# A planned whole-kernel order with eight single PSUM banks: attention reads feeding a max-out FFN on one core

## The chip, the cores and the metric

The kernel runs on one core of one Trainium2 chip. The metric is device time in microseconds for one execution; three executions of the kernel before took 152.25, 152.40 and 152.42 us, a median of 152.4. The profile comes from one more execution. Names of engines: PE is the matmul engine (PEld its weight loads), DVE the vector engine, ACT the scalar engine, POOL the general engine, SP the engine that only issues transfers. POOL also issues transfers, those that change the type among them.

## The reference

Eight batches `b`, eight heads `h`, 512 tokens and 32 states per head, head width 64; then an FFN of width 768 over all 4608 output rows.

```python
scores = scale * np.matmul(x, state.transpose(0, 1, 3, 2))      # [8, 8, 512, 32]
a = softmax(scores)                                             # over the 32 states
xread = np.matmul(a, state)                                     # [8, 8, 512, 64]
a2 = softmax(scale * np.matmul(state, x.transpose(0, 1, 3, 2))) # over the 512 tokens
sread = np.matmul(a2, x)                                        # [8, 8, 32, 64]
x = concat([xread, sread], axis=2) -> [8 * 544, 512]
h = np.maximum(np.maximum(x @ w1, x @ w2), x @ w3)              # 512 -> 768
out = h @ w_out                                                 # 768 -> 512
```

Weights and inputs are float32 in DRAM, and so is the result. The kernel works in bf16 with float32 sums.

## The kernel before, in words

The read of the states is never formed for the 512 tokens of a batch: since `xread @ w = a @ (state @ w)`, the kernel computes `G = state @ w` per batch (32 states by 3 x 768 per head) and multiplies the turned softmax weights `aT` by `G`. Per batch the steps are these, each a small function named by a short word in a table:

- `lx`, `lxg`: load `x` of a batch with a change to bf16 (POOL issues). `xtd`: turn it by a DMA transpose on SP's queue into `xT` (batches 0 and 1 are turned on PE by `xt`, and copied by `xtc`).
- `lst`, `stc`, `stt`, `stp`: load, cast and turn the states of two batches and place them in `bd`, block-diagonal (one `bd` serves two batches). `stt` is four PE transposes.
- `sc`: scores, 16 matmuls with `xT` as weights and `bd` as the moving side. `ex`: exponential on ACT into `e`. `sum`: row sums and reciprocals on DVE. `wt`: the product `a` on POOL. `atd`: DMA transpose of `a` into `aT`.
- `pad`: POOL copies `x` into `xp` with a column of ones between heads. `sr`, `srs`, `srt`, `ap`: the read for the states (`e` as weights, `xp` moving), its scaling on DVE, a DMA transpose, and a copy to its place in `atp`.
- `g`, `gr`, `gq` and `gc`, `grc`, `gqc`: pieces of `G` on PE and their copies out of PSUM on ACT or DVE. Eight matmuls of a piece use eight tiles of 64 x 32 of the PE array at once.
- `l1 b m`: for one of the six 128-wide slices `m` of the FFN, 3 x 2 matmuls of 512 columns into three PSUM banks. `m0` (ACT) casts the first bank, `ma` and `mb` (DVE) take the maximum with the second and the third; `mb` writes `ht`.
- `l2 b j`: six matmuls of 512 columns into one bank, `l2c` copies it to `osb`, `so` stores it. For batch 7 there are narrower pieces (`l2p`, `l2pc`, `sop`).
- `l1s`, `l2 s`: the same for the 256 rows of the states of all batches (256 columns), at the end.
- `look`, `flag`, `vl`: a test that no sum under- or overflowed, and a branch to a slower exact path, which is not taken here. `hold` is a matmul and a copy at the end that keep the branch behind the last work.
- `busy`: matmuls on zeros during the load at the start.

The order of the work is written by hand in a string, `PLAN`: every engine works through its own steps in that order, with waits put in where data or a buffer needs them. Two more strings say which PSUM bank each use takes (`BANKS`) and which SBUF buffer (`PLACES`). Before the change PSUM has four single banks and two pairs; scores and large pieces of `G` take a pair and are copied with one instruction of 1024 columns. In the steady part one batch after another passes with the same pattern: layer 1 of batch `b`, layer 2 of batch `b-1` and the scores and `G` of batch `b+1` interleaved.

Line numbers in the profile before: L249 `busy`, L261 `stt`, L305 `sc`, L313 `ex`, L358 `at`, L391 `sr`, L427 all pieces of `G`, L444, L466 and L469 their copies, L477 layer 1, L492 `m0`, L497 `ma`, L505 `mb`, L514 `l2`, L526 its copy, L532 and L537 the narrower pieces, L543, L548, L541, L556 stores, L591 and L593 `hold`.

Of the kernel before, what the change touches and what calls it, by code (L numbers as in the profile page):

```python
# [9 lines left out]
F32 = mybir.dt.float32  # L10
# [8 lines left out]
    lst 0 A; lxu 0 0 S; zero; clr 0; clr 1; clr 2; clr 3; warm; lxg 0 1; busy 1; xones 1; ident; busy 1;  # L19
    lxg 1 0; busy 1; busy 1; stc 0 D; busy 1; busy 1; busy 1; busy 1; busy 1; lxg 1 1; stt 0; busy 1; busy 1;  # L20
    cxu 0 0 D; xt 0 0; stp 0 A; busy 1; xt 0 1; lw 0 2 1; lw 0 1 0; xtc 0 0 D; sc 0 0; xones 0; lw 0 2 2;
    xtc 0 1 D; busy 1; busy 1; sc 0 1; xt 1 0; ex 0 0; ex 0 1; lw 1 3 0; sum 0 0; sum 0 1; xtc 1 0 A; busy 1;
    busy 1; xt 1 1; sc 1 0; xtc 1 1 D; ex 1 0; busy 1; busy 1; sc 1 1; lw 2 3 2; wt 0 1 D; lw 2 3 1; lw 3 4 0;
    wt 0 0 P; lw 3 6 2; at 0 0; sr 0; ex 1 1; sr 1; g 0 0; sum 1 0; wt 1 0 P; g 1 0; atc 0 0 A; at 0 1; at 1 0;
    gc 0 0 A; atc 0 1 A; g 1 1; sum 1 1; gc 1 0 D; atc 1 0 A; srs 0; srs 1; g 0 1; wt 1 1 P; at 1 1; gc 0 1 A;
    l1 0 0; atc 1 1 D; lst 1 A; m0 0 0; lst 3 A; gc 1 1 A; ma 0 0; lw 3 6 1; lw 4 6 0; lxg 2 1; lxg 2 0; l1 0 1;
    m0 0 1; lwo; mb 0 0; g 0 2; g 1 2; ma 0 1; l1 1 0; lst 2 A; gc 0 2 A; mb 0 1; m0 1 0; ma 1 0; l1 0 2;
    mb 1 0; gc 1 2 A; m0 0 2; ma 0 2; l1 1 1; m0 1 1; g 1 3; stc 1 P; mb 0 2; ma 1 1; g 0 3; mb 1 1; stt 1;
    gc 1 3 A; l1 1 2; gc 0 3 A; m0 1 2; stp 1 DA; ma 1 2; g 0 4; g 0 5; l1 0 3; gc 0 5 D; g 1 4; mb 1 2;
    gc 0 4 A; m0 0 3; gc 1 4 A; ma 0 3; gr 2 1792 2304; mb 0 3; l1 1 3; m0 1 3; grc 2 1792 2304 A; xtd 2;  # L30
    ma 1 3; l1 0 5; stc 2 P; g 1 5; gr 2 0 512; mb 1 3; m0 0 5; ma 0 5; l1 1 4; gc 1 5 A; gr 2 1280 1792;
    m0 1 4; grc 2 0 512 D; mb 0 5; gr 2 512 1024; ma 1 4; grc 2 1280 1792 AD; l1 0 4; m0 0 4; ma 0 4; stt 2;
    mb 0 4; sc 2 -; ex 2 -; grc 2 512 1024 D; stp 2 AD; stc 3 D; mb 1 4; l2 0 3; l2 0 0; l2c 0 3 A; l2c 0 0 A;
    sum 2 -; l2 0 1; ones; pad 2; lxg 3 0; lxg 3 1; wt 2 - P; stt 3; xtd 3; l2c 0 1 A; l1 1 5; pad 3;
    so 0 0 2 P; lx 4; m0 1 5; l2 0 2; ma 1 5; mb 1 5; stp 3 A; l2c 0 2 A; l2 1 0; gq 2 1024 1280; gr 3 0 512;
    gr 3 1792 2304; l2c 1 0 D; grc 3 1792 2304 D; gqc 2 1024 1280 A; grc 3 0 512 A; atd 2; sr 2; l2 1 1; srs 2;
    sc 3 -; l1 2 0; m0 2 0; ex 3 -; l2c 1 1 D; l2 1 3; ma 2 0; gq 3 1024 1280; so 0 2 4 P; gqc 3 1024 1280 A;
    l2c 1 3 A; gr 3 512 1024; gr 3 1280 1792; mb 2 0; sum 3 -; wt 3 - P; atd 3; xtd 4; srt 0; sr 3; srs 3;
    l1 2 1; m0 2 1; ma 2 1; l1 2 2; m0 2 2; mb 2 1; ma 2 2; l1 2 3; m0 2 3; mb 2 2; ma 2 3; l1 2 5; m0 2 5;
    mb 2 3; l2 1 2; grc 3 1280 1792 A; grc 3 512 1024 A; ma 2 5; mb 2 5; l2c 1 2 D; l1 2 4; so 1 2 4 P; m0 2 4;  # L40
    ma 2 4; lx 5; mb 2 4; so 1 0 2 P; pad 4; gr 4 1792 2304; gr 4 0 512; grc 4 1792 2304 AD; l2 2 0; l2 2 1;
# [38 lines left out]
    1032103210 3213201321 0312013201 3201320120 3120132103 1203120312 0310321031 2013210321 0321032132 0132103120  # L80
    1320132103 2103120120 1201320123 0123120123 0213012013 0130123102 2
"""
PAIRS = """
    0101010101 1001010010 0110101010 1010101010 10
"""
PLACES = """
# [657 lines left out]
```

## Time and profile before

| | before |
|---|---|
| time, median of three (lowest to highest) | 152.4 us (152.25 to 152.42) |
| span of the profiled execution, first to last instruction | 150.5 us |
| what lies around the span, median less span | 1.9 us |
| PE busy | 145.1 us, 96% of the span |
| DVE busy | 118.0 us, 78% |
| ACT busy | 83.2 us, 55% |
| POOL busy | 56.1 us, 37% |
| granted PE clock | 1.000 over the span |

The profiled execution's own time is not listed apart from its span; the three timed ones lie 1.75 to 1.92 us above it. How to read it: PE counts as busy from a matmul's start to its modelled end, and matmuls overlap, so that 96% says only that PE seldom stands empty. The chain that ended last, followed back from the end, tells which work has no slack. The windows view cuts the span into stretches and shows for each how long an engine was busy.

### The profile page before, as it was taken

How to read it: one execution, taken by the hardware profiler on the slowest of the kernel's cores; microseconds unless marked ns; L12 is line 12 of the kernel's file. 1: busy time of each engine (PE TensorE's matmuls, PEld its weight loads, DVE VectorE, ACT ScalarE, POOL GpSimd, SP SyncE). 2: the span in 40 equal slices, each digit the busy share in tenths (PEclk: the TensorE clock that was granted, in tenths of full speed). 3: DMA queues.
4: the chain of work that ended last, by engine and by line, in shares of the span. 5: the costliest groups of instructions: out<-in, count | busy, mean ns of one | idle time of the engine just before them, and what ended most of it. 6: DMA issues, size and time to landing. Idle time of an engine off the chain costs nothing.

```text
span 150.5 us, 3618 instructions
## 1 busy us (share of the span) xinstructions
PE 145.1 (96%) x1422; PEld 72.8 (48%) x1422; DVE 118.0 (78%) x202; ACT 83.2 (55%) x144; POOL 56.1 (37%) x78
## 2 busy tenths in 40 slices
PE   6998999999999999999999999999999999999991
PEld 2556443335444443444344434443444446689770
DVE  6488788999967899789978997899789888674443
ACT  3366888965654574457546764676466653332220
POOL 6996911090392507350735064506250200001500
PEclk9999999999999999999999999999999999999999
DMA  4999999949647996998399839983303340300555
GB/s 121 195 188 189 206 230 198 196 97 139 124 97 171 235 182 189 108 209 178 145 102 216 183 139 90 231 183 131 157 4 78 121 175 7 139 0 17 190 199 167
DMA packets 39108, 22.29 MB, mean 148 GB/s; under 512 B 23072, under 2 KB 36896, under 8 KB 39088
## 3 DMA queue, kind: packets, MB, share of 16 engines
q0 software_dynamic: 15872, 13.96, 49.3%
q1 hardware_dynamic: 21632, 6.69, 22.8%
q10 hardware_dynamic: 1584, 1.38, 3.2%
q8 instruction: 12, 0.20, 0.6%
q14 instruction: 8, 0.07, 0.2%
HBM read 15.20 MB, written 8.91 MB: 160 GB/s over the span
## 4 chain that ended last, share of the span: by engine, by line
PE 88%; DMA 5%; POOL 3%; issue 1%; DVE 1%; ACT 1%; POOLq 0%
PE pw L477 47%; PE po L514 25%; PE pg L427 6%; DMA w<-in_moe_w_dram 5%; PE po L532 4%; PE ps L305 2%; PE psr L391 2%; POOL w L217 1%; POOL x L206 1%; PE pgh L427 1%; ACT G L444 1%; PE pt L261 1%; DVE held L593 0%; PE idle L591 0%; PE pat L358 0%
## 5 line engine op out<-in xcount | busy, mean ns | idle before, releaser
L477 PE MATMUL pw<-aT,G 128*128 128x512 bf16 x288 | 66.7, 379 | 0.0
L492 ACT CAST t<-pw 128x512 bf16<-128x512 f32 (+1 forms) x54 | 30.5, 564 | 27.3 <-PE pw L477 26.4
L497 DVE TENSOR_TENSOR t<-t,pw 128x512 bf16<-128x512 bf16 (+1 forms) x54 | 35.3, 654 | 11.1 <-ACT t L492 8.9
L477 PEld LDWEIGHTS <-G 128*128 128x128 bf16 x288 | 27.1, 98 | 32.8 <-issue 2.1
L514 PE MATMUL po<-wout,ht 128*128 128x512 bf16 x168 | 39.7, 379 | 0.0
L505 DVE TENSOR_TENSOR ht<-t,pw 128x512 bf16<-128x512 bf16 x48 | 32.9, 686 | 4.5
L349 POOL TENSOR_TENSOR a<-e,rden 128x1024 bf16<-128x1024 bf16 (+1 forms) x9 | 14.6, 1622 | 27.2 <-ACT osb L526 11.1
L514 PEld LDWEIGHTS <-ht 128*128 128x128 bf16 x168 | 15.4, 98 | 19.0 <-issue 1.7
L548 POOL DMA_DIRECT2D out_dram<-osb x13 | 7.4, 571 | 27.5 <-ACT t L492 27.5
L466 ACT CAST G<-pg 128x1024 bf16<-128x1024 f32 (+1 forms) x17 | 14.7, 895 | 2.1 <-PE pg L427 2.1
L526 ACT COPY osb<-po 128x512 f32<-128x512 f32 x15 | 8.9, 592 | 9.1 <-PE po L514 9.1
L526 DVE COPY osb<-po 128x512 f32<-128x512 f32 x14 | 9.6, 688 | 3.9 <-PE po L514 3.8
L375 POOL COPY xp<-x 128x1024 bf16<-128x1024 bf16 x12 | 12.3, 1059 | 0.0
L313 ACT ACTIVATE e<-ps 128x1024 bf16<-128x1024 f32 (+1 forms) x10 | 8.5, 854 | 6.7 <-PE ps L305 6.7
L466 DVE CAST G<-pg 128x1024 bf16<-128x1024 f32 (+1 forms) x12 | 11.6, 995 | 0.0
L342 DVE TENSOR_REDUCE seen<-e 128x32 f32<-128x1024 bf16 (+1 forms) x10 | 10.0, 997 | 1.7 <-ACT e L313 1.7
L427 PE MATMUL pg<-w,bd 64*32 64x512 bf16 (+1 forms) x288 | 10.7, 362 | 0.4 <-DMA w<-in_moe_w_dram 0.2
L444 ACT CAST G<-pg 128x768 bf16<-128x768 f32 x10 | 8.0, 810 | 2.7 <-PE pg L427 2.5
L543 POOL DMA_DIRECT2D out_dram<-osb x4 | 2.2, 544 | 19.4 <-ACT osb L537 19.4
L249 PE MATMUL idle<-zero 128*128 128x512 bf16 x18 | 7.4, 506 | 1.8 <-DVE zero L225 1.3
L477 PE MATMUL pw<-atp,w 128*128 128x256 bf16 x72 | 8.7, 272 | 0.0
L217 POOL DMA_DIRECT2D w<-in_moe_w_dram x10 | 7.7, 782 | 0.0
(70 smaller groups left out, 112.1 us busy)
## 6 DMA issues: line engine op xcount, KB each, us to landing
out_dram<-osb POOLq DMA_DIRECT2D x12, 512.0 KB, 3.7
x<-in_x_dram POOLq DMA_DIRECT2D x4, 512.0 KB, 7.2
x<-in_x_dram POOLq DMA_DIRECT2D x7, 256.0 KB, 5.8
w<-in_moe_w_dram POOLq DMA_DIRECT2D x4, 256.0 KB, 7.5
w<-in_moe_w_dram POOLq DMA_DIRECT2D x2, 384.0 KB, 7.5
wout<-in_moe_w_out_dram POOLq DMA_DIRECT2D x1, 768.0 KB, 12.0
out_dram<-osb SPq DMA_DIRECT2D x3, 256.0 KB, 2.4
stf<-in_state_dram ACTq DMA_DIRECT2D x4, 128.0 KB, 5.3
```

What stands on the lines that cost most here:

```text
L342: nc.vector.reduce_sum(out=den, in_=parity(e[b], g), axis=AX.X)
L349: times[c](out=parity(a[b], g).rearrange("p j g s n -> p j (g s) n"), in0=parity(e[b], g).rearrange("p j g s n -> p j (g s) n"), in1=rdens ...
L375: nc.gpsimd.tensor_copy(out=xp[b][:, :, :, g * (D + 1):g * (D + 1) + D], in_=v[:, g])
L427: nc.tensor.matmul(p(s, g), bd(b, 2 * s + g)[64 * g:64 * g + 64, g, :], f(w_sb[64 * g:64 * g + 64, s]), start=True, stop=True, tile_positi ...
L444: copier[c[g]](out=G[b][:, g:h, :, m * 128:m * 128 + 128], in_=p[:, g:h, 0:384].rearrange("p g (i f) -> p g i f", i=3))
L466: copier[c[g]](out=v[:, g:h], in_=p[:, g:h, 0:c1 - c0])
L477: nc.tensor.matmul(pw[i][:, 0:n], lhs(i, k), rhs(k), start=(k == 0), stop=(k == nk - 1))
L492: nc.scalar.copy(out=t0s[b, m][:, 0:n], in_=open_ps["l", b, m][0][:, 0:n])
L497: nc.vector.tensor_max(t1s[b, m][:, 0:n], t0s.pop((b, m))[:, 0:n], open_ps["l", b, m][1][:, 0:n])
L505: nc.vector.tensor_max(ht[b][:, m, :], t1s.pop((b, m))[:, 0:n], open_ps.pop(("l", b, m))[2][:, 0:n])
L514: nc.tensor.matmul(p, ht[b][:, m, tokens(b, j)], wout_sb[:, m, :], start=(m == 0), stop=(m == NM - 1))
L526: copier[c[i]](out=o[:, j, i * w:i * w + w], in_=p[:, i * w:i * w + w])
```

## The change

The functions change little, the three tables wholly. What it does:

- PSUM is eight single banks. Scores and pieces of `G` take two of them, and each is copied by its own instruction (512 or 384 columns where 1024 or 768 stood).
- Batches 5, 6 and 7 are scored the other way round (`sq`, `eq`, `etd`): `bd` are the weights and `xT` moves, 16 matmuls on eight 64 x 32 tiles, so that states lie on the partitions; the exponential goes to `eT`, and a DMA transpose on SP makes `e`.
- States 4 to 7 are turned by a DMA transpose on SP (`std` for `stt`), and placed by DVE and POOL.
- `x` of batches 5, 6 and 7 is loaded by three transfers that POOL issues one after another.
- The flag's matmul and test come earlier; batch 7 is put out in seven pieces (sixteen quarter-tiles in twelve before), the first half of the states in one (two before).
- The first loads of weights are smaller; `xp` has two columns of ones.

```diff
 PLAN = """
-    lst 0 A; lxu 0 0 S; zero; clr 0; clr 1; clr 2; clr 3; warm; lxg 0 1; busy 1; xones 1; ident; busy 1;
...
+    lxg 0 1; lxu 0 0 S; zero; busy 1; lst 0 A; busy 1; busy 1; warm; busy 1; stc 0 A; busy 1; cxu 0 0 A; ident;
...
 BANKS = """
-    0123012301 2230210020 1121020310 2321302130 1203102301 2310213012 3120132132 3102301230 2301203103 2103120132
...
-PAIRS = """
...
+    0123456701 2345670234 5610275634 0721653075 1263471052 6731067450 2316475167 0253461374 2065174036
...
     def bank(shape, dtype, name):
-        return pp.tile(shape, dtype, tag="b" + next(homes["b"]), bufs=1, name=name)
-
-    def two_banks(shape, dtype, name):
-        return pp.tile(shape, dtype, tag="w" + next(homes["w"]), bufs=1, name=name)
+        return pp.tile(shape, dtype, tag="b" + next(homes[0]), bufs=1, name=name)
...
     def exps(b, g=None):
         new(e, b, [128, J, 2, HS, Ns], "e")
-        nc.scalar.activation(
-            out=parity(e[b], g).rearrange("p (c i) g s n -> p i c (g s n)", i=2),
-            in_=open_ps.pop(("s", b, g)).rearrange("p (i c) g s n -> p i c (g s n)", i=2),
-            func=AF.Exp, scale=scale)
...
+            for i in range(2):
+                nc.scalar.activation(
+                    out=out[:, i], in_=ps[i].rearrange("p c g s n -> p c (g s n)"), func=AF.Exp, scale=scale)
...
     def scores_turned(b):
-        p = open_ps["sq", b] = two_banks([128, 2, 2, 2, 128], F32, "pst")
+        ps = open_ps["sq", b] = [bank([128, 2, 2, 128], F32, "pst") for _ in range(2)]
         for g in range(2):
             for s in range(HS):
                 for c in range(2):
                     nc.tensor.matmul(
-                        p[32 * s:32 * s + 32, c, :, g, :], bd(b, 2 * s + g)[64 * c:64 * c + 64, c, :],
+                        ps[c][32 * s:32 * s + 32, :, g, :], bd(b, 2 * s + g)[64 * c:64 * c + 64, c, :],
                         xT[b][64 * c:64 * c + 64, 2 * s + g, :, :],
                         start=(g == 0), stop=(g == 1), tile_position=(64 * c, 32 * s), skip_group_check=True)
...
     def g_run(b, c0, c1):
+        ps = open_ps["g", b, c0] = [bank([128, 512], F32, "pg") for _ in range(2)]
+        g_mm(b, lambda s, g: ps[g][32 * s:32 * s + 32, 0:c1 - c0],
              lambda v: v.rearrange("p i f -> p (i f)")[:, c0:c1])
...
     def g_ran(b, c0, c1, c):
         new_g(b)
+        v = G[b].rearrange("p g i f -> p g (i f)")
+        for g, p in enumerate(open_ps.pop(("g", b, c0))):
+            copier[c[g % len(c)]](out=v[:, g, c0:c1], in_=p[:, 0:c1 - c0])
```

What the new table moves is shown at three places. The first is POOL at the start: its loads of `x` (x_82 and x_83 are batches 0 and 1) and of the three weight matrices (`w`; 128x4x128 is one 128-wide slice of one matrix), and its products `a`. Before:

```order
L206 DMA x_83<-in_x_dram 128x4x256 x2
L217 DMA w<-in_moe_w_dram 128x4x256
L217 DMA w<-in_moe_w_dram 128x4x128
L236 MEMSET x_82 128x64
L217 DMA w<-in_moe_w_dram 128x4x256 x2
L217 DMA w<-in_moe_w_dram 128x4x128 x3
L349 TENSOR_TENSOR a<-e,rden 128x4x128
L217 DMA w<-in_moe_w_dram 128x4x384
L349 TENSOR_TENSOR a<-e,rden 128x4x128 x2
L217 DMA w<-in_moe_w_dram 128x4x384
L217 DMA w<-in_moe_w_dram 128x4x256
```

Now, at the same place on POOL:

```order
L199 DMA x_83<-in_x_dram 128x4x256 x2
L210 DMA w<-in_moe_w_dram 128x4x128 x2
L210 DMA w<-in_moe_w_dram 128x4x256
L210 DMA w<-in_moe_w_dram 128x4x128 x3
L210 DMA w<-in_moe_w_dram 128x4x256
L353 TENSOR_TENSOR a<-e,rden 128x4x128
L210 DMA w<-in_moe_w_dram 128x4x128 x2
L353 TENSOR_TENSOR a<-e,rden 128x4x128 x2
L210 DMA w<-in_moe_w_dram 128x4x384
L210 DMA w<-in_moe_w_dram 128x4x256 x2
```

The three transfers that the first piece of `G` needs are four slices together where they were five; the transfers behind the products are one of 384 and two of 256 where they were two of 384 and one of 256, of which one stood between the products.

The second place is DVE in layer 1 of batch 2 (t1 is written by `ma`, ht by `mb`, osb by the copy of layer 2, sr by `srs`). Before, each slice's two maxima follow each other:

```order
L497 TENSOR_TENSOR t1_1035<-t0_1033,pw1_1025 128x512
L505 TENSOR_TENSOR ht_976<-t1_1035,pw2_1026 128x512
L497 TENSOR_TENSOR t1_1049<-t0_1046,pw1_1038 128x512
L505 TENSOR_TENSOR ht_976<-t1_1049,pw2_1039 128x512
L497 TENSOR_TENSOR t1_1063<-t0_1060,pw1_1052 128x512
L505 TENSOR_TENSOR ht_976<-t1_1063,pw2_1053 128x512
```

Now, on DVE in layer 1 of the same batch:

```order
L487 TENSOR_TENSOR t1_1071<-t0_1054,pw1_1046 128x512
L516 COPY osb_898<-po_977 128x512
L495 TENSOR_TENSOR ht_1085<-t1_1071,pw2_1047 128x512
L487 TENSOR_TENSOR t1_1087<-t0_1083,pw1_1059 128x512
L487 TENSOR_TENSOR t1_1093<-t0_1091,pw1_1075 128x512
L495 TENSOR_TENSOR ht_1085<-t1_1087,pw2_1060 128x512
L495 TENSOR_TENSOR ht_1085<-t1_1093,pw2_1076 128x512
L487 TENSOR_TENSOR t1_1126<-t0_1108,pw1_1100 128x512
L487 TENSOR_TENSOR t1_1140<-t0_1119,pw1_1111 128x512
L495 TENSOR_TENSOR ht_1085<-t1_1140,pw2_1112 128x512
```

The maxima of different slices are mixed, and a copy of layer 2 stands inside a slice. In the new plan PE meets eight slices of layer 1 in a row there (six of batch 2 and two of batch 3, with the scores of batch 4 among them); before there were at most four.

The third place is the end of ACT, before it reads the flag. Before:

```order
L537 COPY osb_2313<-po_2417 128x128
L543 DMA out_0_dram<-osb_2313 128x128
L537 COPY osb_2434<-po_2427 128x256
L537 COPY osb_2313<-po_2438 128x256
L543 DMA out_0_dram<-osb_2313 128x256
L543 DMA out_0_dram<-osb_2313 128x128 x2
```

Now, at the end of ACT (osb_2480 is the states' output, osb_2434 that of batch 7):

```order
L531 DMA out_0_dram<-osb_2480 32x4x512
L527 COPY osb_2434<-po_2492 128x384
L527 COPY osb_2434<-po_2500 128x256
L533 DMA out_0_dram<-osb_2434 128x256
L533 DMA out_0_dram<-osb_2434 128x128
```

The last two copies of the kernel are now both on ACT, and a store that waits for a copy on DVE stands ahead of them; before, the last copies were on DVE.

More of the change, by code (lines that the diff above doesn't have):

```diff
@@ L34 @@
[L34 to L38, printed above, removed]
@@ L165 @@
     open_ps = {}
-    homes = {n: iter("".join(t.split())) for n, t in (("b", BANKS), ("w", PAIRS))}
+    homes = [iter("".join(BANKS.split()))]
     places = {}
@@ L385, in sread @@
                     if b in xp:
-                        both = xp[b][:, s, j, g * D:g * D + D + 1]
+                        both = xp[b][:, s, j, g * (D + 1):g * (D + 1) + D + 1]
                     else:
```

236 lines of the change are left out of this document (115 added, 121 removed), and 3 rows, old and new, of the table BANKS.

## The prediction

> **What bounds the kernel now.** I read the page first (busy shares, chain by engine), then the windows by batch, then the chain in order of time, then the engines' own order in one batch.
>
> The page's first lines and its chain by engine; below them the windows view (columns: stretch, length, busy us and instructions of PE, PEld, DVE, ACT, POOL, granted clock, share of the DMA engines, GB/s) for the start and one batch of the steady part:
>
> ```profile
> span 150.5 us, 3618 instructions
> PE 145.1 (96%) x1422; PEld 72.8 (48%) x1422; DVE 118.0 (78%) x202; ACT 83.2 (55%) x144; POOL 56.1 (37%) x78
> PE 88%; DMA 5%; POOL 3%; issue 1%; DVE 1%; ACT 1%; POOLq 0%
> ```
>
> ```profile
> 0.00:15.90 15.90, 13.67 (x199) 7.68 (x200) 11.11 (x24) 8.31 (x14) 13.19 (x24) 1.00 1.24 174
> 79.79:95.03 15.24, 15.24 (x149) 6.81 (x150) 12.88 (x21) 9.06 (x16) 6.03 (x7) 1.00 0.83 157
> ```
>
> PE is 88% of the chain. In the steady batch PE is full, DVE has 12.88 of 15.24 us, ACT 9.06, POOL 6.03. So the end is set by three things: when PE's unbroken run begins, how much it holds, and what follows it. The chain in order of time (start us, length us, what) gives all three, and the price of each kind of PE work:
>
> ```profile
> 6.06 7.41 DMA w<-in_moe_w_dram
> 15.55 0.33 PE pat L358 x4
> 15.88 2.59 PE pw L477 x12
> 34.06 0.22 PE pt L261 x4
> 38.64 0.22 PE pt L261 x4
> 61.74 0.47 PE ps L305 x16
> 63.50 0.23 PE pgh L427 x8
> 63.73 0.43 PE pg L427 x16
> 64.54 5.30 PE pw L477 x24
> 135.09 0.33 PE po L532 x6
> 136.74 2.97 PE po L532 x36
> 142.34 0.66 PE po L532 x6
> 144.29 2.67 PE po L532 x36
> 146.95 0.02 issue
> ```
>
> The first layer-1 slice starts at 15.88, PE runs without a break of note to 146.95, and 3.55 us follow to the span's end at 150.5. Before the run, the chain is the third load of weights, 7.41 us from its issue to its landing at 13.47.
>
> **The change, part by part.** I work it out against the span of 150.5; the median is 1.9 us more (what lies around the span), which I leave as it is.
>
> *Start.* The first piece of `G` waits for three loads. They and the loads ahead hold one slice of one matrix less (128 KB in bf16), and that is also the difference up to the fifth load, which the last piece ahead of layer 1 needs. The transfers between 10 and 20 us in the DMA view:
>
> ```profile
> DMA packets 4397, 1.98 MB, mean 198 GB/s; under 512 B 2168, under 2 KB 4396, under 8 KB 4396
> ```
>
> At 198 GB/s, 128 KB are 0.65 us. Before, four transposes of `a` (0.33, the row at 15.55) stood ahead of layer 1; now batch 1's eight stand behind its first slice. So layer 1 begins 0.65 + 0.33 = 0.98 earlier, and 0.66 come into the run: net -0.32. Bounds: 0 if ACT's and DVE's copies, not the weights, hold the first slice (then only the order of the transposes changes), -0.98 if the transposes behind the first slice fill a wait.
>
> *Turning of states.* Eight PE transposes go, two rows of 0.22: -0.45. Instead SP issues two transposes, and DVE and POOL place them. The states' loads land long before, and `bd` of batches 4 and 5 is first needed at a piece of `G` some 2 us of PE work after SP is through; cost zero, else the lateness of SP below.
>
> *Scores of 5, 6, 7.* 16 matmuls of 64 columns with 128 x 128 weights go, 0.47 each batch. In come 16 of 256 columns on eight tiles at once. No such row exists before; the nearest is the pair of large `G` pieces in the same tiling, 16 of 512 columns in 0.43, so half the columns are 0.22. All three stand directly ahead of `G` pieces of the same 64 x 32 tiling, so no change of tiling comes with them. 3 x (0.47 - 0.22) = -0.75; the other bound is zero, if a tile's two sums run one after the other without overlap.
> What follows them is longer: two exponentials, a transpose on SP, then sums, product, transpose of `a`. With these rows (page and DMA issues):
>
> ```profile
> L313 ACT ACTIVATE e<-ps 128x512 bf16<-128x512 f32 x4 | 2.4, 597 | 2.5 <-PE ps L305 2.5
> L342 DVE TENSOR_REDUCE seen<-e 128x32 f32<-128x1024 bf16 x6 | 7.3, 1217 | 1.4 <-ACT e L313 1.4
> L349 POOL TENSOR_TENSOR a<-e,rden 128x1024 bf16<-128x1024 bf16 x6 | 11.4, 1908 | 25.8 <-ACT osb L526 11.1 <-ACT t L492 6.1 <-DVE seen L401 4.7
> xT<-x SPq DMA_TRANSPOSE x6, 5.3
> aT<-a SPq DMA_TRANSPOSE x6, 2.9
> ```
>
> 2 x 0.6 + 2.9 (the transpose of `e` has `a`'s eight blocks) + 1.2 + 0.35 + 1.9 + 2.9 = 10.5 us from the scores to a batch's first slice. Between them the new PE order has, for batch 5, ten slices of layer 1 or 2 (12.9), thirteen pieces of `G`, the other scores and four reads for the states: over 16 us. So this costs nothing unless SP is late.
>
> *Output.* The narrow pieces cost 0.33 + 2.97 + 0.66 + 2.67 = 6.63 for 84 matmuls. The new ones: three of 128 at 0.33, one of 256 at 0.66, one of 384 at 0.99, three of 512 (one the states') at 1.29, half of the twelve matmuls in 2.59: 6.51, so -0.12. That narrow pieces are no dearer by column than wide ones is what these rows show.
>
> *Changes of tiling.* 24 layer-1 matmuls behind `G` and `sr` take 5.30, twelve alone 2.59: 0.12 on leaving a tiled group, and as much on entering (eight of 256 columns 0.23, where half of the next row's 0.43 per eight would be 0.11). Counting the groups behind the first slice, 16 become 17: +0.24.
>
> *Single banks.* The copies of 1024 columns become two of 512. From the groups by form:
>
> ```profile
> L466 ACT CAST G<-pg 128x1024 bf16<-128x1024 f32 x12 | 11.7, 1024 | 0.0
> L466 DVE CAST G<-pg 128x1024 bf16<-128x1024 f32 x7 | 8.5, 1217 | 0.0
> L466 DVE CAST G<-pg 128x512 bf16<-128x512 f32 x5 | 3.4, 684 | 0.0
> L526 DVE COPY osb<-po 128x512 f32<-128x512 f32 x14 | 9.6, 688 | 3.9 <-PE po L514 3.8
> ```
>
> A copy in two costs DVE 2 x 0.684 - 1.217 = 0.15 more, ACT (by the exponential's 0.597, also 512 columns out of PSUM) 2 x 0.597 - 1.024 = 0.17. On DVE, seven copies of 1024 and two of 768 become twelve of 512 and ten narrower ones, some 3 us more; its output copies fall from 14 of 0.69 and seven narrow ones to 12, some 3 us less, so DVE keeps its 118. ACT gets 18 split copies (3 us) and five more output copies, less what DVE and POOL take from it: some 5 more, 88 of 150. Neither total binds; what can bind is a stretch, below.
>
> *Flag early, `x` of 5 to 7 together.* The flag's matmul only moves. The three loads are issued while POOL has 25.8 us of idle time ahead of its products (the row of L349), and the scores that need the first of them come some 20 us of PE work later. Zero both.
>
> *End.* Before, the last narrow copies were 0.29 on DVE and the last store landed 1.8 after its issue. Now ACT copies 384 and then 256 columns and issues two stores, and a store of 768 KB from POOL starts some 4 us earlier. The rows that bear on it:
>
> ```profile
> L537 ACT COPY osb<-po 128x256 f32<-128x256 f32 x3 | 1.1, 374 | 0.7 <-PE po L532 0.7
> out_dram<-osb POOLq DMA_DIRECT2D x12, 512.0 KB, 3.7
> out_dram<-osb ACTq DMA_DIRECT2D x3, 64.0 KB, 1.8
> ```
>
> The copy is 0.08 longer and the last store stands behind another (about 0.3 of issue): between -0.4 (eight last stores where there were fourteen) and +0.8 (the large store in the way); I take +0.3, what the two rows give.
>
> *New waits.* The states' load (issue to landing), and SP's queue (start, time that it holds SP):
>
> ```profile
> stf<-in_state_dram ACTq DMA_DIRECT2D x4, 128.0 KB, 5.3
> ```
>
> ```profile
> 80.39 2.97 SPq L291 DMA_TRANSPOSE xT<-x  x1
> 83.46 1.25 SPq L366 DMA_TRANSPOSE aT<-a  x1
> 84.80 1.19 SPq L410 DMA_TRANSPOSE ats<-sr  x1
> ```
>
> The states of 2 and 3 are loaded one transfer later on ACT and turned earlier, by the start's 0.98 and some 0.9 of PE work. The load takes 5.3, so `stt` may wait 0 to 0.5. SP is fuller: between the transposes of `x` of 5 and 6 stand two small ones and, ahead, that of `a` of 4. SP holds 2.97 for each `x`, 1.25 for `a`, 1.19 for each small one: 2 x 2.97 + 2 x 1.19 + 1.25 = 9.6, and 2.3 more to landing; PE has some 11 us of work from the product `a` of batch 4 to the scores of batch 6. Just short: 0 to 1. For all new waits I take +0.4, between 0 and 3.1 (the DVE case below).
> [...]
>
> Sum: -0.32 - 0.45 - 0.75 - 0.12 + 0.24 + 0.3 + 0.4 = -0.7. Span 149.8, time **151.7 us**.
>
> **The rivals.**
>
> *The start is given back* (about no change). The weights of the fourth slice come in a transfer that POOL issues only after its products `a` of batch 1, as before. If that load, not PE, sets when those pieces of `G` run, PE waits there for what it gained (0.65 to 0.98). For it: the start's window has the DMA engines full (share 1.24). Against: the queue ahead is shorter. Time: 152.4 - 0.7 + 0.7 = 152.4.
>
> *Slower: DVE in two long runs of layer 1.* Three steps of DVE in a steady batch (start, length), and the group of the first reduction of `look`:
>
> ```profile
> 65.73 0.69 DVE L497 TENSOR_TENSOR t<-t,pw 128x512 bf16<-128x512 bf16 x1 [0.42 <-ACT t L492]
> 66.53 0.69 DVE L505 TENSOR_TENSOR ht<-t,pw 128x512 bf16<-128x512 bf16 x1
> 67.13 0.68 DVE L497 TENSOR_TENSOR t<-t,pw 128x512 bf16<-128x512 bf16 x1
> ```
>
> ```profile
> L566 DVE TENSOR_REDUCE top<-seen 128x1 f32<-128x272 f32 x1 | 0.4, 427 | 0.0
> ```
>
> Eight slices and one set of scores in a row in batches 2 and 3 are 8 x 1.29 + 0.47 = 10.8 of PE; DVE has 16 maxima, a copy and a scaling, 16 x 0.685 + 0.69 + 0.4 = 12.0. Ten in a row in batches 5 to 7 are 12.9 of PE against 20 x 0.685 + 1.15 (`look`: two reductions of 0.43 and two small tests) = 14.85. The excess is 1.2 + 1.9 = 3.1. Eight banks hold two slices and two thirds, so a part is absorbed, but DVE enters the first run with sums and copies of `G` still to do. What decides is DVE's pace from start to start, in the rows above 0.80 where `mb` needs the `ma` ahead of it, 0.60 where it doesn't. The new order mixes slices, so most steps should take 0.60, and then 16 of them are 9.6 and the run fits. If the pace stays 0.685 or worse, the price is 3.1 less 0.8 that the banks take: 151.7 - 0.4 + 2.3 = 153.6.
> [...]
>
> *Faster: nothing new waits.* All terms but the end and the waits are -1.4, and 0.4 of the start's other 0.66: 150.6. For it: PE is the chain in 88%, and the mixed order suits DVE. Against: every queue is fuller.
>
> **How the numbers follow.** Forecast 151.7 (its own range 151.0 to 152.1): 0.42. Faster still, 150.6: 0.14. No change, 152.4: 0.17. Slower, 153.6: 0.27. Within 0.2%, 0.3 us, nothing can be told from no change. So faster 0.56, same 0.17, slower 0.27. The range for 8 in 10 reaches from the gain with no waits, the start at its bound and the end 0.4 shorter, 152.4 - 1.4 - 0.66 - 0.4 = 149.9, to the DVE case in which the banks take only 0.5, 151.3 + 2.6 = 153.9.
>
> **What would show it.** Right: the chain's first layer-1 slice near 14.9; rows of `pst` of 0.2 to 0.25 for 16; PE's run ending near 146 and 3.8 us behind it; steps of 0.60 between DVE's maxima. Wrong: PE idle or waiting on DVE between 48 and 60 or 100 and 115 us; PE waiting on the weights near 21; a transposed `x` or `e` that lands after PE asks for it; DMA engines full to the last microsecond.

## The result: 5.6% slower, and the profile after

| | before | after |
|---|---|---|
| time, median (lowest to highest) | 152.4 us (152.25 to 152.42) | 160.7 us (159.99 to 161.81, four executions) |
| ratio, with its 95% interval | | 1.056 (1.051 to 1.061) |
| span of the profiled execution | 150.5 us | 159.6 us (its own time 161.35) |

The forecast was 151.7, its range ended at 153.9. Some kernels below have executions far above their fastest; the ratios leave those out, and there the text gives lowest and highest. The page of the changed kernel: its first lines, PE's busy tenths and the granted clock in forty slices of 4 us, and the chain by engine.

```profile
span 159.6 us, 3543 instructions
PE 147.2 (92%) x1381; PEld 71.2 (45%) x1381; DVE 112.2 (70%) x204; ACT 86.2 (54%) x170; POOL 56.8 (36%) x79
...
PE   6999999999999999999998942899999999999980
...
PEclk9999999999999999999999998589999999999999
...
PE 78%; DMA 8%; ACT 3%; DVE 3%; POOL 2%; SPq 2%; issue 1%; ACTq 0%; DVEq 0%
```

PE has a hole in slices 23 to 25, counted from 0, and just behind it the clock falls. PE's own rows there (start, length, group; in brackets its idle time before and what ended it), its first slice of layer 1 and its last output:

```profile
14.92 1.46 PE L467 MATMUL pw<-aT,G 128*128 128x512 bf16 x6
...
87.25 0.41 PE L326 MATMUL pst<-xT,bd 64*32 64x256 bf16 x16 [0.55 <-DMA xT<-x]
...
98.42 1.07 PE L395 MATMUL psr<-xp,e 128*32 128x65 bf16 x64 [4.90 <-DMA e<-eT]
100.16 6.49 PE L467 MATMUL pw<-aT,G 128*128 128x512 bf16 x18 [0.67 <-DMA aT<-a]
...
152.93 1.79 PE L522 MATMUL po<-wout,ht 128*128 128x384 bf16 x12
```

And the windows around it (as in the prediction, the clock is the third number from the end):

```profile
96.00:100.00 4.00, 1.07 (x64) 0.91 (x64) 0.86 (x4) 0.00 (x0) 1.72 (x1) 0.79 1.13 170
100.00:104.00 4.00, 3.84 (x10) 1.37 (x11) 1.68 (x3) 0.21 (x1) 2.09 (x2) 0.50 0.15 34
104.00:108.00 4.00, 4.00 (x18) 1.70 (x17) 3.04 (x7) 2.13 (x5) 0.23 (x1) 0.86 0.34 78
```

These rows make up the 9.1 us of span:

- Start: first slice at 14.92 for 15.88, -0.96.
- Waits: 0.55 for `xT` of batch 7, 4.90 for `e` of batch 7, 0.67 for `aT` of batch 5: +6.12.
- Clock: the first 18 matmuls of layer 1 of batch 5 take 6.49. At 0.216 each (2.59 for twelve before) they'd take 3.89: +2.60. The reads ahead of them take 1.07, where the kernels below at full clock have 0.72; these 0.35 are in the last line.
- End: from PE's last output (152.93 + 1.79 = 154.72) to the span's end 4.88, before 3.55: +1.33.
- All other work of PE: from first slice to last output 139.80, before 131.07; less 6.12 and 2.60, 0.0 (and -0.35 without the reads' clock).

Why the transposes are late stands first in SP's queue (start, time that SP is held):

```profile
78.07 1.75 SPq L339 DMA_TRANSPOSE e<-eT  x1
79.92 4.12 SPq L284 DMA_TRANSPOSE xT<-x  x1
84.08 3.21 SPq L414 DMA_TRANSPOSE ats<-sr  x2
87.34 0.58 SPq L538 DMA_DIRECT2D out_dram<-osb  x1
88.01 1.10 SPq L414 DMA_TRANSPOSE ats<-sr  x1
89.22 4.65 SPq L339 DMA_TRANSPOSE e<-eT  x2
93.92 5.05 SPq L370 DMA_TRANSPOSE aT<-a  x2
```

SP is held almost without a break from 78 to 99. The transposes of `e` of 6 and 7 come at 89.2, behind `x` of 7, three small transposes and a store; that of `a` of 5 comes behind them, at 93.92. POOL's product for it was done at 87.54, 6.4 us earlier. The transfers from 88 to 101 us, in forty steps of 0.325 us, with the times from issue to landing, and POOL's rows, its product `a` of batch 5 and its issue in the middle:

```profile
GB/s 0 265 384 244 14 0 0 136 206 106 0 0 1 9 9 186 406 403 403 403 416 392 423 429 251 228 129 117 210 170 256 207 223 54 269 95 104 286 103 0
...
out_dram<-osb POOLq DMA_DIRECT2D x2, 512.0 KB, 4.4
...
e<-eT SPq DMA_TRANSPOSE x2, 6.3
aT<-a SPq DMA_TRANSPOSE x2, 4.7
```

```profile
85.63 1.91 POOL L353 TENSOR_TENSOR a<-e,rden 128x1024 bf16<-128x1024 bf16 x1 [5.99 <-DVE seen L405]
...
91.53 1.11 POOL L538 DMA_DIRECT2D out_dram<-osb  x2
```

POOL issues 1 MB of stores at 91.5, and from 93 to 96 us the engines move about 400 GB/s, while the three transposes that PE needs are under way; `e` of 6 and 7 and `a` of 5 take 4.8, 7.7 and 6.2 us (before, `aT` took 2.9). So after the result there were four candidates: SP's order, POOL's stores, POOL's pads (which the chain of waits names between 87.6 and 91.6), and the order of PE and DVE behind the late thing.

### The profile page after: what moved, and what is told of

The parts are those of the page before. It is cut to its first block, busy times and chain, and to the rows that moved or that the text cites. A ratio compares the mean times of both kernels' runs of the same rounds, so it can differ in the third digit from the quotient of the medians.

```text
span 159.6 us, 3543 instructions
## 1 busy us (share of the span) xinstructions
PE 147.2 (92%) x1381; PEld 71.2 (45%) x1381; DVE 112.2 (70%) x204; ACT 86.2 (54%) x170; POOL 56.8 (36%) x79
## 4 chain that ended last, share of the span: by engine, by line
PE 78%; DMA 8%; ACT 3%; DVE 3%; POOL 2%; SPq 2%; issue 1%; ACTq 0%; DVEq 0%
PE pw L467 43%; PE po L504 19%; PE pg L431 5%; DMA xT<-x 5%; DMA aT<-a 4%; PE idle L242 4%; PE po L522 3%; POOL xp L379 2%; SPq L339 2%; PE ps L303 1%; DVE seen L346 1%; PE psr L395 1%; PE pat L362 1%; ACT bd L264 1%; PE pst L326 1%
## 5 line engine op out<-in xcount | busy, mean ns | idle before, releaser
L459 ACT CAST G<-pg 128x512 bf16<-128x512 f32 (+1 forms) x39 | 19.5, 561 | 2.9 <-PE pg L431 2.8
L516 ACT COPY osb<-po 128x512 f32<-128x512 f32 x19 | 11.2, 588 | 12.1 <-PE po L504 12.0
L459 DVE CAST G<-pg 128x512 bf16<-128x512 f32 (+1 forms) x21 | 12.5, 629 | 2.3 <-PE pg L431 2.2
L538 POOL DMA_DIRECT2D out_dram<-osb x11 | 6.1, 558 | 20.7 <-DVE osb L516 12.5
L431 PE MATMUL pg<-w,bd 64*32 64x512 bf16 (+2 forms) x336 | 12.0, 350 | 0.1
L419 POOL COPY atp<-ats 128x128 bf16<-128x128 bf16 x4 | 1.9, 465 | 21.9 <-DMA ats<-sr 21.8
L210 POOL DMA_DIRECT2D w<-in_moe_w_dram x12 | 9.1, 783 | 0.0
L447 ACT CAST G<-pg 128x384 bf16<-128x384 f32 x18 | 7.7, 490 | 1.7 <-PE pg L431 1.6
L516 DVE COPY osb<-po 128x512 f32<-128x512 f32 x10 | 6.7, 685 | 1.7 <-PE po L504 1.7
L467 PEld LDWEIGHTS <-w 128*128 128x128 bf16 x72 | 7.0, 98 | 1.7
```

Source lines behind the costliest of these rows:

```text
L431: nc.tensor.matmul(p(s, g), bd(b, 2 * s + g)[64 * g:64 * g + 64, g, :], f(w_sb[64 * g:64 * g + 64, s]), start=True, stop=True, tile_positi ...
L459: copier[c[g % len(c)]](out=v[:, g, c0:c1], in_=p[:, 0:c1 - c0])
L467: nc.tensor.matmul(pw[i][:, 0:n], lhs(i, k), rhs(k), start=(k == 0), stop=(k == nk - 1))
L516: copier[c[i]](out=o[:, j, i * w:i * w + w], in_=p[:, i * w:i * w + w])
```

## The experiments

All kernels are edits of the changed one, and its line numbers hold. The time is the median; the ratio is to the kernel before, 152.0 to 152.3 in the same sessions.

### What the hole is

**hole_busy**

```diff
+    busy 20;   # ahead of
     sr 7; sr 6;
```

> Twenty matmuls on zeros (4.3 us at 0.215 each) stand between the last piece of G of batch 7 and the read for the states of batch 7, where PE stands empty for 4.9 us; nothing else changes. Theory (the hole has two prices, the wait for the transposes and the clock that falls while PE is empty): the matmuls cost nothing, the granted clock stays at 1.00 from 100 to 104 us (0.50 in the changed kernel), the first 18 matmuls of layer 1 of batch 5 take 3.9 instead of 6.49, and the time falls by 2.5 to 3.5 us, to 157.2 to 158.2 from 160.7. Rival (those matmuls are slow because their operands come late, not for the clock): no change, 160 to 161.8. If the transposes landed later for it: slower.

157.9, ratio 1.040 (1.037 to 1.042). PE's rows:

```profile
94.82 4.49 PE L242 MATMUL idle<-zero 128*128 128x512 bf16 x19
99.46 0.72 PE L395 MATMUL psr<-xp,e 128*32 128x65 bf16 x64
100.11 4.06 PE L467 MATMUL pw<-aT,G 128*128 128x512 bf16 x18
```

The read isn't earlier (99.46 for 98.42), yet it takes 0.72 for 1.07, the 18 matmuls take 4.06, not 6.49, and 2.7 us are gone. The granted clock is 1.00 from 100 to 104 us, where it was 0.50. The clock is a price of its own, on top of the wait.

**old_scores**

```diff
-    sq b; eq b; etd b;         # b = 5, 6, 7
+    sc b -; ex b -;
-    e ... 5:0 6:1 7:0;
+    e ... 5:0 6:2 7:1;
```

> Batches 5, 6 and 7 are scored as before the change (xT as weights, exponential straight into e, no transpose of e on SP); the buffer of e for batch 6 and 7 is a third one and the second, so that ACT needn't wait for the read of batch 4. Everything else is the changed kernel's. Theory (the transposes of e on SP's queue, with what stands ahead of and behind them, make the hole): PE gains 3 x 0.25 = 0.75 us of matmuls, the hole of 6.1 us and the slow clock's 2.6 go, 152.5 to 154.0. Rival (the late x of 7 or the stores make the hole, with or without e): a hole of at least 4 us stays between 85 and 104 us, 157 or more. Rival (the single banks or the new order elsewhere cost the time): 158 or more, with no hole there.

152.96, ratio 1.006 (1.003 to 1.009): 7.7 us hang on the turned scores and their three transposes of `e`.

```profile
93.62 0.72 PE L395 MATMUL psr<-xp,e 128*32 128x65 bf16 x64
94.27 4.06 PE L467 MATMUL pw<-aT,G 128*128 128x512 bf16 x18
```

The read and layer 1 follow without a gap: without the turned scores there is no hole. The single banks, the turned states and the three loads together are all in this kernel, and make none. Of the 0.9 us left over the kernel before, another end gives back 0.6 (below).

### What makes the transposes late

**xt7_early, stores_late, stores_xt7**: each cause alone, then both.

```diff
-    ...; etd 5; ...; xtd 7;
+    xtd 6; xtd 7; ...; etd 5;                                # xt7_early, stores_xt7
-    l1 5 5; so 3 2 4 P; ...; so 2 2 4 P; ...; wt 7 - P;
+    l1 5 5; ...; wt 7 - P; so 3 2 4 P; so 2 2 4 P;           # stores_late, stores_xt7
```

> The transpose of x of batch 7 is issued directly behind that of batch 6 (near 74 us) instead of behind the transpose of e of batch 5 (79.9); nothing else moves. Theory (SP's queue in its order makes e of 6 and 7 late): e of 5, which stood ahead of it, is issued up to 3 us later, the four small transposes, the store and e of 6 come up to 4 us earlier, e of 7 some 2 us earlier (it then waits for its scores and for the product of batch 5), and the hole shrinks from 4.9 by 2 to 3.5 us: 156.0 to 158.5, the slow clock included. Rival (POOL's pads 7 and 6 hold back e of 7, as the chain names them): e of 7 is issued no earlier than 91.6, and the time stays within 0.7 us of 160.7.

155.1 (154.5 to 155.9, and one execution at 165.6); ratio 1.021 (1.017 to 1.025). One place on SP is worth 5.6 us in most executions, more than expected. The profile is of the one at 165.6 and doesn't show the usual one: there `e` of batch 5, now behind `x` of 7, makes PE wait 2.85 us at its read, and `aT` of 5 another 4.77.

> POOL issues the two stores of 512 KB (batches 3 and 2, second halves) behind its product of batch 7 (after 100 us) instead of at 91.5; nothing else moves. In the changed kernel the DMA engines move nothing from 91.4 to 92.3, then 420 GB/s to 95.9, while the transposes of e of 6 (issued at 89.2), e of 7 (90.7) and a of 5 (93.9) are under way. Theory (those stores, issued and moved in the middle of the transposes, hold them up): e of 7 lands near 95 instead of 98.4, aT of 5 near 96 instead of 100.1, the hole shrinks by 3 to 4 us and the clock falls less: 155.0 to 157.5. Rival (the order on SP alone, or POOL's pads, set when e of 7 is issued and lands): within 0.7 us of 160.7.

156.0 (154.4 to 157.3), ratio 1.022 (1.015 to 1.029). The same window as above, and PE, in the execution at 157.3:

```profile
e<-eT SPq DMA_TRANSPOSE x2, 4.6
aT<-a SPq DMA_TRANSPOSE x2, 2.8
```

```profile
95.74 0.72 PE L395 MATMUL psr<-xp,e 128*32 128x65 bf16 x64 [1.61 <-DMA e<-eT]
96.73 5.75 PE L467 MATMUL pw<-aT,G 128*128 128x512 bf16 x18 [0.27 <-DMA aT<-a]
```

With nothing changed on SP, `e` lands in 4.6 for 6.3 and `aT` in 2.8 for 4.7: the stores did hold the transposes up, by 1.7 and 1.9 us at the median. How the transfers of POOL and of SP share the engines isn't shown.

> Both moves: the two stores late, and the transpose of x of batch 7 directly behind that of batch 6. The second alone gave 155.1 in most executions and 165.6 in one. Theory (two causes in one chain, SP's order ahead of e of 6 and 7 and the stores behind it): the hole falls below 1 us and stays there, 151.5 to 153.5, with no execution over 155. Rival (the early transpose of x of 7 collides with others whatever the stores do): the spread of several us stays.

155.0 (154.3 to 155.5), ratio 1.019 (1.015 to 1.023): the spread is gone as expected, the time is not. The two gains don't add. Part of what is left shows on other engines:

```profile
84.34 0.31 DVE L419 COPY atp<-ats 128x128 bf16<-128x128 bf16 x1 [3.07 <-DMA ats<-sr]
```

```profile
85.01 0.58 ACT L516 COPY osb<-po 128x512 f32<-128x512 f32 x1 [3.19 <-DMA out_dram<-osb]
```

A small transpose and a store now stand behind `x` of 7 on SP; DVE and ACT wait 3 us each for them, with copies of `G` and maxima behind. PE's own waits between 84 and 97 us are short, 0.92 and 0.32 for `e` and 0.35 for a copy of `G`; another part is the end, which this kernel still has as changed (4.87 us behind PE's last output, 3.77 in `queues_3` below). This run also clears POOL's pads: SP is done with both transposes of `e` at 92.16 (89.47 + 2.69), the pads run to 93.91 (91.90 + 2.01).

```profile
89.47 2.69 SPq L339 DMA_TRANSPOSE e<-eT  x2
```

```profile
91.90 2.01 POOL L379 COPY xp<-x 128x1024 bf16<-128x1024 bf16 x2
```

**sp_relief**

```diff
-    ...; so 1 0 1 S; so 1 2 4 S; ...; so 1 1 2 S; ...; srt 0; ...; srt 1; so 0 0 1 S;
     so 0 2 4 S;                                                                   # at 52 us
+    srt 0; srt 1; so 1 0 1 S; so 1 2 4 S; so 1 1 2 S; so 0 0 1 S;
```

> Six issues of SP whose data has been ready since 15 to 50 us (the small transposes of the states' reads of batches 0 and 1, and four stores of batches 0 and 1, 5.9 us of SP's time between 74 and 88 us) go to SP's idle time behind 52.6 us. Nothing else moves; the transposes of e stay, and so do POOL's stores at 91.5. Theory (SP works in order and is full from 66 to 100 us, so that what stands ahead of the transposes of e and a is what PE waits for): e of 6 is issued near 83 to 85 instead of 89.2, e of 7 as soon as its exponential is done (89) instead of 90.7 to 91.6, a of 5 near 91; PE's wait at the read for batch 7 falls from 4.9 to 1 to 2.5, the clock holds better, 153.5 to 156.5. Rival (POOL's stores and the engines' traffic at 92 to 96 alone decide): 159 or more.

160.2, ratio 1.055 (1.052 to 1.058): no better than the change. But the waits are others:

```profile
73.56 4.06 PE L467 MATMUL pw<-aT,G 128*128 128x512 bf16 x18 [2.23 <-DMA aT<-a]
...
96.26 0.71 PE L395 MATMUL psr<-xp,e 128*32 128x65 bf16 x64 [0.19 <-DMA e<-eT]
99.63 5.75 PE L467 MATMUL pw<-aT,G 128*128 128x512 bf16 x18 [2.66 <-DMA aT<-a]
```

The wait for `e` fell from 4.90 to 0.19, but only half of that is the theory's: `e` was there 2.2 us earlier (96.26 for 98.42), and PE came to the read 2.5 us later (96.06 for 93.53). The wait came back twice: for `aT` of 5 (with POOL's stores beside it again), and at 71 us for `aT` of 4. The stores had gone among the loads of `x` of 5 to 7, which then landed after 15.2 us, and the transposes of `a` beside them after 5.4; in the changed kernel they took 9.0 and 2.7:

```profile
x<-in_x_dram POOLq DMA_DIRECT2D x3, 512.0 KB, 15.2
```

So the rival that SP alone decides falls too: SP's idle time is not free time of the DMA engines.

### What stands behind the late transposes

**reads_late, all_moved, all_moved_2**

```diff
-    etd 6; ...; sum 6 -; ...; etd 7; ...; sr 7; sr 6; atd 5; l1 5 5; ...; l1 5 2; ...; l1 5 1; l2 4 1;
+    atd 5; etd 6; ...; etd 7; ...; l1 5 5; ...; l1 5 2; ...; l1 5 1; sr 7; l2 4 1; sr 6;    # all three
     # all_moved: sum 6 behind the maxima of 5; stores_xt7's moves
     # all_moved_2: sum 6 ahead of them; moves of sp_relief and stores_xt7, another end
```

> PE does the reads for the states of batches 7 and 6 behind three slices of layer 1 of batch 5 instead of ahead of them (their scalings on DVE move with them, two maxima of batch 5 come earlier to free a bank), and SP issues the transpose of a of batch 5 ahead of the two of e. All work stays. Theory (layer 1 of batch 5 waits for nothing it needs, only for what stands ahead of it on PE and on SP): a of batch 5 is ready at 87.5, its transpose lands near 93, PE begins layer 1 near 93.5 and has 5 us of work until e of 7 lands; the hole shrinks from 6.1 to below 1.5, the clock holds, 152.0 to 154.0. Rival (the transposes are slow for the stores on the DMA engines, wherever they stand): aT of batch 5 lands after 96, the hole keeps 2.5 or more, and the time is 155.5 or more.

162.9, ratio 1.076 (1.070 to 1.082), slower than the change. The theory that only PE's and SP's order are in the way fell:

```profile
98.11 1.22 DVE L346 TENSOR_REDUCE seen<-e 128x32 f32<-128x1024 bf16 x1 [6.20 <-DMA e<-eT]
```

```profile
100.11 6.05 PE L467 MATMUL pw<-aT,G 128*128 128x512 bf16 x18 [6.40 <-DVE G L459]
```

`aT` of 5, now issued at 89.47, landed 4.9 later and held nobody. But DVE does the sums of batch 6 ahead of two copies of `G`, and stood 6.2 us for `e`; the banks that layer 1 wants are freed by those copies. With the reads out of the way the same lateness came through DVE.

> Four moves together: the two stores late, the transpose of x of 7 early, that of a of 5 ahead of those of e of 6 and 7 with the reads for the states of 7 and 6 behind three slices of layer 1 of batch 5, and on DVE the sums of batch 6 behind the copies of the last pieces of G. With the third alone (162.9) the hole stayed, since DVE waited 6.2 us for e of 6 and the copies of G behind it held the banks that layer 1 needed. Theory (each thing that is late stands in the way of work that doesn't need it): PE meets no wait above 0.5 us from 75 to 109, 151.3 to 153.0. Rival (the transposes themselves are too slow for this order): over 154.

161.7, ratio 1.060 (1.057 to 1.064), against 151.3 to 153.0 expected. Layer 1 of batch 5 now starts at 97.89 without a wait, but the edit puts the sums of batch 6 behind four maxima, so the product and `aT` of batch 6 came late:

```profile
110.20 2.31 PE L467 MATMUL pw<-aT,G 128*128 128x512 bf16 x5 [4.37 <-DMA aT<-a]
```

The profile is of its longest execution, 165.09. There PE also waits 2.79 us for `e` of batch 5 at 87.7, which stands behind `x` of 7 as in `xt7_early`.

> As the last one, and the reads for the states of 7 and 6 behind three slices of layer 1 of batch 5, with the transpose of a of 5 ahead of those of e of 6 and 7, and the sums of batch 6 on DVE behind the last copies of G but ahead of the maxima of batch 5 (in the earlier kernel with four moves they stood behind them, and a of batch 6 was 5 us late for it). Theory (with every late thing out of the way of what doesn't need it no wait is left): 151.0 to 152.2. Rival (the chain e, sums, product, a of batch 6 is now the late one): 153 or more, with PE waiting for aT of batch 6 near 105.

156.4, ratio 1.029 (1.026 to 1.033), against 151.0 to 152.2 expected. Its profile has only this wait on a transpose above 0.4 us, and from 75 us on none:

```profile
73.80 5.75 PE L467 MATMUL pw<-aT,G 128*128 128x512 bf16 x18 [2.09 <-DMA aT<-a]
```

2.1 of wait and 1.7 of clock, both from `sp_relief`'s stores.

### The end

**old_scores_end, old_scores_end2**

```diff
-    so 6 0 3 P;                            # behind l2c 6 2
+    so 6 0 2 P; ... so 6 2 3 P;            # behind l2c 6 0, and behind l2c 6 2
-    sop s 0 0 512 A; ...
+    sop s 0 0 512 S;                       # behind sos 1 S
     # old_scores_end2: also sop 7 0 0 128 on S for A, and sp_relief's moves
```

> The kernel with the old scores (152.96) with another end: the store of 768 KB of batch 6 in two, 512 KB some 2.8 us earlier and 256 KB where it was, and the store of the first half of the states issued by SP instead of by ACT ahead of ACT's last two copies. From PE's last output matmul to the end of the span the changed kernel takes 5.0 us, the one before 3.55. Theory (ACT's issue of a store delays its last copies by 0.5 and the large store is still moving when the last small ones want to): 0.8 to 1.5 us less, 151.5 to 152.2. Rival (the end is the last stores' own time from issue to landing): within 0.3 us of 152.96.

152.34, ratio 1.001 (0.999 to 1.003). 0.6 less than `old_scores` (0.7 by the ratios), below the 0.8 expected. ACT's last rows, first with the old end, then with the new:

```profile
145.54 0.65 ACTq L531 DMA_DIRECT2D out_dram<-osb  x1
146.23 0.75 ACT L527 COPY osb<-po 128x384 f32<-128x384 f32 x2 [1.90 <-PE po L522]
```

```profile
145.55 0.48 ACT L527 COPY osb<-po 128x384 f32<-128x384 f32 x1 [1.46 <-PE po L522]
146.20 0.37 ACT L527 COPY osb<-po 128x256 f32<-128x256 f32 x1 [0.18 <-PE po L522]
```

ACT no longer issues a store ahead of its last two copies, and the last ends at 146.57 for 146.98. Of these 0.41, PE's own last output is 0.25 earlier (146.16 for 146.41). Which part of the 0.6 is ACT's and which the split store's wasn't tried apart.

> The kernel with the old scores and the other end (152.34), with the six issues of SP early and the last small store of batch 7 on SP instead of behind another on ACT. Theory (ACT issues two stores one behind the other at the very end, 0.86 us): 0.2 to 0.5 less, 151.8 to 152.2; the issues of SP do nothing here, since PE waits for no transpose. Rival: within 0.2 of 152.34.

154.9, ratio 1.015 (1.012 to 1.019), 2.5 worse: the stores moved to 52 us make PE wait 1.66 us for `aT` of batch 4 in the profile, with the old scores as well. The expectation that they do nothing here was wrong; on the last small store the run says nothing.

### All causes away

**sp_relief_end, all_moved_3, queues_3, old_scores_3**: the first has the moves of `sp_relief` and `stores_xt7` (with the copy that DVE waited on put later) and the other end. The other three have the stores of batches 0 and 1 ahead of the loads of `x`:

```diff
+    xtd 4; so 0 2 4 S; so 1 0 2 S; so 0 0 1 S; ...; atd 3; so 1 2 4 S; srt 0; srt 1;
     # queues_3: with all else of sp_relief_end
     # all_moved_3: queues_3 with the reads late; old_scores_3: queues_3 with the old scores, xtd 7 where it was
```

> The six issues early, and with them: the transpose of x of 7 directly behind that of 6 (the copy on DVE that waited for the small transpose behind it goes later), POOL's two stores behind its product of batch 7, and the end changed (the store of 768 KB in two, the last store of the states and the small one of batch 7 on SP instead of ACT). Theory: no wait on a transpose above 1 us is left, the turned scores keep their gain of about 0.4 in PE's time, and the end gives 0.6 to 1.0: 151.3 to 152.6, near the kernel before (152.2). Rival (the transposes of e are too slow for these places whatever stands ahead): 153.5 or more.

154.8, ratio 1.018 (1.016 to 1.020): one wait above 0.5 us is left, of 1.99 us, for `aT` of 4, with the clock behind it:

```profile
72.77 5.75 PE L467 MATMUL pw<-aT,G 128*128 128x512 bf16 x18 [1.99 <-DMA aT<-a]
```

> The same queues of SP and POOL and the same end, but the reads for the states of 7 and 6 stand ahead of layer 1 of batch 5 as in the changed kernel, and the sums of batch 6 ahead of the copies of G. Theory: a wait of 0.5 to 1.5 us for e of 7 and for the copy of G is left, too short for the clock: 151.6 to 153.3, some 0.5 above all_moved_3. Rival (place of the reads decides): 154 or more.

152.25 (151.0 to 156.5, twelve executions), ratio 0.998 (0.995 to 1.001). Every instruction of the turned scores is still there, and 8.4 us are gone, some 0.6 of them by the other end:

```profile
span 150.2 us, 3533 instructions
```

```profile
93.51 0.71 PE L395 MATMUL psr<-xp,e 128*32 128x65 bf16 x64 [0.29 <-DMA e<-eT]
94.30 4.06 PE L467 MATMUL pw<-aT,G 128*128 128x512 bf16 x18
...
144.64 1.79 PE L522 MATMUL po<-wout,ht 128*128 128x384 bf16 x12
```

> As the second kernel with all moves (156.4), but four stores of batches 0 and 1 go to 49 to 52.5 us, ahead of the loads of x of 5 to 7, not among them. There PE waited 2.1 us for aT of batch 4 and the clock then cost 1.7, and after 75 us it met no wait on a transpose. Theory (the late transposes and the clock that falls behind them are the whole loss): 151.0 to 152.8. Rival (the turned scores cost something of their own, or the stores collide here too): 153.5 or more.

153.0 (152.2 to 158.3), ratio 1.004 (1.002 to 1.006): no better than `queues_3` with the reads in their old place, against the expected 0.5 in its favour. Its profiled execution took 156.96, with 2.63 us of PE's waiting for `aT` of batch 3 at 59 us.

> The old scores with the same early stores and small transposes of SP, POOL's stores late and the changed end; the transpose of x of 7 where the changed kernel has it. Theory: PE waits for nothing, 151.8 to 152.3 (152.34 with the old queues, less 0 to 0.4 for the last store), and all_moved_3 is 0.2 to 0.5 below it, which is the turned scores' worth (0.47 - 0.34 for each of three in the rows). Rival (turned scores are worth nothing or cost): old_scores_3 is level with all_moved_3 or below.

152.2 (151.3 to 159.2), ratio 1.000 (0.998 to 1.003), level with `queues_3`. A gain of the turned scores, expected at 0.2 to 0.5, doesn't show.

**queues_4, old_scores_4**: the stores of batch 0 at 38 us, to calm the spread.

```diff
-    xtd 4; so 0 2 4 S; so 1 0 2 S; so 0 0 1 S;
+    xtd 3; so 0 0 1 S; so 0 2 4 S; ...; xtd 4; so 1 0 2 S;
```

> As queues_3, but the two stores of batch 0 (768 KB) go to 38 to 42 us, where SP and the DMA engines have room, so that ahead of the transpose of a of batch 3 only one store of 512 KB stands. Theory (the spread of queues_3 is that transpose's landing, late in some executions): 151.2 to 152.0, and hardly an execution over 153. Rival (the spread comes from the crowd of transposes at 70 to 100 us): the same 152.2 with the same spread.

154.7 (152.7 to 157.5, six executions), ratio 1.011 (1.005 to 1.018): worse, not steadier.

> The same queues with the old scores. Theory: 151.7 to 152.3, 0.2 to 0.6 over queues_4 (three times 0.47 - 0.34, and the transposes' entry into the tiling). Rival: level with it.

157.1 (152.2 to 159.7): the ratio of 1.003 (0.999 to 1.007) rests on four of thirteen executions. The profile of the one at 157.9:

```profile
61.36 2.56 PE L467 MATMUL pw<-aT,G 128*128 128x512 bf16 x6 [3.08 <-DMA aT<-a]
```

`aT` of batch 3 is late here too, and this kernel has no transpose of `e`. In this profile (157.9) and in that of `all_moved_3` (156.96) the long wait lies among the loads, stores and transposes between 38 and 65 us, not in the crowd at 70 to 100. Which of them collide in which execution stays open. No version beat the kernel before; `queues_3`, `old_scores_3` and `old_scores_end` equal it.

## Why the prediction was wrong, step by step

**The failed step is "this costs nothing unless SP is late", with "just short: 0 to 1" for SP.** It had three errors.

- *The cover waited itself.* The way from the scores to a batch's first slice was put at 10.5 us against 16 us of PE work, and among this work I counted "four reads for the states". Two of them, of batches 7 and 6, are the first things that need the late `e`, and stand ahead of layer 1 in PE's order. The 4.90 us are spent there. `reads_late` showed the same on DVE, with the sums ahead of copies of `G`.
- *SP was added up for one transpose only.* I stopped at `x` of 6. Behind it stand `e` of 5, `x` of 7, three small ones, a store, `e` of 6 and 7, and only then `a` of 5: SP's rows above from 78 to 99 us. For batch 5 the way from the scores (75) to the first slice (100.2) took 25 us, not 10.5: 12.8 to the end of its product (part of this is the planned order of other engines), 6.4 for its turn on SP, 6.2 to land.
- *Times from issue to landing were those of a quieter queue.* I took 2.9 for a transpose of 256 KB and 5.3 for `x`. With POOL's stores beside them, `e` took 6.3 and `a` 4.7 at the median; `stores_late` shows that the stores' part is 1.7 to 1.9 each. `x` of 7, issued at 79.9, ahead of those stores, took 7.2, and 7.4 in `stores_late`; its cause wasn't tried.

The new waits were put at +0.4, at most 3.1 with DVE; they were 6.12, and both ends of that bound had been built for another mechanism. No rival had the transposes of `e` in it, though "a transposed `x` or `e` that lands after PE asks for it" stood among the signs.

**The clock was left out.** The granted clock was 1.00 in every window before, and I took it as given. It cost 2.95 us in the profile (2.60 in layer 1, 0.35 in the reads) and 2.7 by `hole_busy`.

**The end** was +0.3 within -0.4 to +0.8, and measured +1.33. The mechanism was named (the large store in the way), but not ACT's issue ahead of its last two copies. The other end returned 0.6; the rest stays open.

**The start** came out: 14.92 for 14.9. That it fits so closely is partly luck: the other kernels, with the same start, have their first slice between 14.46 and 15.45. If 0.66 of it went into the run, as forecast, the other terms there were about -1.0, for the rest of -0.35; they were put at -1.08, and the next paragraph takes 0.36 of that away, so 0.3 isn't accounted for.

**The turned scores' own gain** was half the size: 16 matmuls took 0.34 (the row at 74.84 in the chain below), not 0.22, against 0.47, so -0.39 for three, not -0.75. `queues_3` against `old_scores_3` can't tell even that from nothing.

**DVE's two long runs**, the slower rival, didn't happen: 42 and 60 matmuls of layer 1 in a row run at 0.218 and 0.216 each, in the changed kernel's chain in order of time (in `queues_3`, with no hole ahead in which DVE could catch up, 60 take 13.11):

```profile
49.37 9.17 PE pw L467 x42
...
74.84 0.34 PE pst L326 x16
...
109.24 12.95 PE pw L467 x60
```

**The start given back** didn't happen either: PE waits for no weights between 15 and 30 us. And **with nothing new waiting**, forecast at 150.6, `queues_3` is at 152.25: even without the lateness the change is worth nothing that shows. The 150.6 had the scores at their full 0.75 and the end at no cost; the profile of `queues_3` has the first slice at 15.26, a run of 131.17 to PE's last output (131.07 before) and 3.77 behind it (3.55 before).

## What to carry to other kernels

When a step moves onto a queue that works in order, as SP's did here (`a` of 5 was done 6.4 us before its turn), write down everything that stands on this queue until the last thing that is needed, each with its measured hold and with the traffic beside it, not only the next entry. Work counts as cover only if neither it, nor anything ahead of it on its engine, needs the thing it is to cover (the two reads here: 4.90 us). A gap on PE costs its length and, as four of the five gaps of 1.99 to 4.90 us in the first sentence of the next section did here (1.7 to 2.6 us), the clock behind it too; and idle time of an issuing queue isn't idle time of the transfer engines (in `sp_relief` three loads of `x` landed after 15.2 us for 9.0).

## What the hardware showed that I had not expected

PE's gaps and the 18 matmuls of 512 columns behind them (4.06 at a granted clock of 1.00 in `hole_busy`): an unbroken gap of 1.99 us and of 2.09 made them 5.75, one of 2.23 left them at 4.06, one of 2.66 made them 5.75, and 4.90 with 0.67, around the reads, made them 6.49. In `stores_late` 1.61 with 0.27 around the reads made them 5.75, in `old_scores_end2` an unbroken 1.66 left them at 4.06. So the price of the clock in layer 1 is 0 or 1.7 us near 2 us of gap, and 2.6 at 5 (against the 3.89 worked out above), and nearly equal gaps may or may not pay it. The granted clock shows what is paid: its mean is 0.989 over the 153.6 us of `sp_relief_end`, whose one such gap is that of 1.99, and so 1.7 us are lost there; in the changed kernel it is, by windows of 1 us, 0.64 from 98 to 99, 0.50 to 105 and 0.94 to 106, twice that. What decides whether a gap near 2 us pays it isn't shown.

SP's hold for one and the same transpose isn't fixed: `x` holds it 1.33 to 6.29 us (the most in `sp_relief`), `e` 1.24 (in `xt7_early`) to 3.54 (in `reads_late`). What sets it when several follow each other isn't settled by these runs; nor is why the engines moved next to nothing (0 to 10 GB/s) from 91.3 to 92.9 us with two transposes issued, in the changed kernel and, without POOL's stores, in `stores_late` too (0 to 9 from 91.9 to 93.2).
